# A searched order of steps replaced by another: same steps and buffers, other ORDER, SLOTS, ENGS and WARM tables

## The chip, the cores and the metric

The kernel runs on one core of a Trainium2 chip. A core has five engines with instruction streams of their own: TensorE (PE, matrix multiplication), VectorE (DVE), ScalarE (ACT), GpSimd (POOL) and SyncE (SP), which here only issues DMAs. Sixteen DMA engines move the data. The metric is the device time of one execution in microseconds (us). A profile of one further execution shows when each instruction ran on its engine.

## What is computed

Attention with a window, for 4 batches of 8 heads with 768 tokens and 64 elements a head, then a feed-forward layer on the 3072 tokens of 512 elements. The reference, cut to what matters:

```python
scores = scale * np.matmul(q, k.transpose(0, 1, 3, 2))
keep = is_global | is_local            # first 8 keys, and the last 96
scores = np.where(keep, scores + bias, -1000000000.0)
a = np.exp(scores - max); a = a / (np.sum(a) + 1e-09)
x = np.matmul(a, v)                    # heads side by side: 3072 x 512
...
h = x @ w_in                           # 512 -> 1024
solu = h * softmax(h)
ln = (solu - mean) / np.sqrt(var + 1e-06) * g_ln
return ln @ w_out                      # 1024 -> 512
```

## The kernel before

The kernel first writes down a plan: 1115 steps, each with the engines that may do it, what it depends on, which buffers it takes and frees, and a function that emits its instructions. Four tables at the top of the file then say all that the plan leaves open. ORDER is a permutation of the step numbers, and instructions are emitted in this order; so it fixes what stands behind what in each engine's stream, in SyncE's stream of DMA issues too. SLOTS gives the buffer that each step takes out of its pool, ENGS the engine where several may do a step, and WARM where matmuls that compute nothing are put in to keep TensorE busy. The tables were found by a search outside the file that plans with a duration for each step. Nothing of the search is in the file, and an engine waits for whatever its next instruction needs, at whatever time that comes.

```python
for n, i in enumerate(ORDER.split()):
    s = self.steps[int(i)]
    s["slot"] = [(t, int(next(slots))) for t in s["take"]]
    s["warm"] = warm.get(n, [])
    out.append(s)
```

The work of one batch, by steps and by the lines that the profile names:

- *Loads.* SyncE issues the DMAs for k and q of a pair of heads (L478, in batch 3 L485), v (L492, with its ends at L500 and its first rows at L507), the weights w_in (L608, four parts, into the buffer `late`) and w_out (L618, four parts). An engine casts them to 16 bits (L266 on ScalarE, L268 on VectorE, L270 on GpSimd).
- *Turning k and q.* In batches 0 to 2 TensorE transposes them (L726) and ScalarE or VectorE copies them from PSUM (L266, L268). In batch 3 SyncE issues DMA transposes for them (L760, tiles kT and qT), one for k and one for q of each of four pairs. The first 8 keys of every pair go through a small GpSimd step into the tile kg (L522).
- *Attention.* Scores by TensorE (L872, bias L858; the first keys L924 and L930), exponentials by ScalarE (L880, L937), sums (L951, L960), their logarithms (L967) spread by L1011 and exponentiated (L1020), the product with v (L1045, L1055), and the scaled result xT on VectorE (L1080). In batches 1 to 3 VectorE multiplies the exponentials by a factor (L888).
- *First layer.* For each of 24 tiles of 128 tokens eight matmuls of 512 columns (L1114) into two PSUM banks, ef = exp on ScalarE (L1120), then u = ef times the sum on VectorE (L1123), which frees the banks; squares of u on ScalarE (L1130) or VectorE (L1134). There are three buffers for u (uu0 to uu2) and two for ef.
- *Second layer.* u is transposed, for tiles 5 to 21 by a DMA that SyncE issues (L1139, into `late`), for the others by TensorE (L1149) and a copy; a buffer of u is free when its square and its transpose are done. Then eight matmuls of 512 columns (L1195), scaling (L1205 on ScalarE, L1208 on VectorE), and the store (L1212), issued by SyncE or ScalarE.
- *Weights.* w_out is scaled (L631, L637), and its mean (L644) taken off (L648) before the second layer.

Matmuls of line L1221 are those of WARM. SyncE's stream is the queue that the change's name speaks of: its DMA issues run one after the other, and an issue that has to wait holds up all behind it.

Of the kernel before, what the change touches and what calls it, by code (L numbers as in the profile page):

```python
# [28 lines left out]
FACT = {1, 2, 3}  # L29
SPLIT = False  # L30
ORDER = """
# [31 lines left out]
"""  # L63
SLOTS = """
# [10 lines left out]
"""  # L75
ENGS = """
# [4 lines left out]
"""  # L81
WARM = """
18:0:5 30:1:4 34:2:5 44:3:1 47:4:7 52:5:3 74:2:2 118:1:5 131:4:1 152:7:1 161:7:1 167:7:1
"""


# [1173 lines left out]
```

## Time and profile before

| what | us |
|---|---|
| median of 3 runs | 161.38 |
| lowest and highest run | 161.08 and 162.39 |
| the profiled execution's own time | 161.28 |
| its span, first to last instruction | 159.6 |

In the profile the span is the time from the first instruction of the program to the last; the run's time has 1.7 us around it. PE, DVE, ACT and POOL are the engines as above, PEld is TensorE's loading of weights, SPq is SyncE's queue of issues. The busy share of an engine is an average over stages; what bounds a stage is read from what its engines waited for there. The page's digits are busy tenths in 40 slices of 4 us.

### The profile page before, as it was taken

The page shows a single profiled execution, that of the slowest core. Times are in us where ns is not written, and L with a number is a line of the kernel's source. Part 1 is how long each engine was busy: PE and PEld are TensorE (multiplying, and loading weights), DVE is VectorE, ACT ScalarE, POOL GpSimd, SP SyncE. Part 2 cuts the span into 40 slices and gives each one's busy share as a digit, 9 for nine tenths or more (in the row PEclk, how much of TensorE's full clock was granted, in tenths as well). Part 3 has the DMA queues.
Part 4 walks back from the last instruction along what each step waited for, and adds up shares of the span by engine and source line. Part 5 has one row for each costly group of instructions (what it writes and reads, how often), then busy time and mean ns, then how long its engine had stood idle before and what let it go on. Part 6 is the DMA issues. An engine that isn't in the chain of part 4 may idle for free.

```text
span 159.6 us, 4825 instructions
## 1 busy us (share of the span) xinstructions
PE 147.4 (92%) x1893; PEld 79.8 (50%) x1893; DVE 114.0 (71%) x256; ACT 130.5 (82%) x219; POOL 56.4 (35%) x127
## 2 busy tenths in 40 slices
PE   5797989997999999999999799689999999999991
PEld 1454555455664556664444456334546644444550
DVE  6824778599998996889949976866975474728500
ACT  3949998999999799979897599768996679886531
POOL 7583935728756096400543042261040400000000
PEclk9999999999999999999999999999999999999998
DMA  4899989999999999999998999889972965681333
GB/s 152 249 347 331 317 229 359 349 373 334 366 313 263 217 193 266 257 193 205 246 186 180 242 189 191 164 217 198 227 236 82 172 148 113 184 229 66 134 138 131
DMA packets 74519, 35.85 MB, mean 225 GB/s; under 512 B 63608, under 2 KB 70016, under 8 KB 74496
## 3 DMA queue, kind: packets, MB, share of 16 engines
q1 hardware_dynamic: 73776, 34.22, 90.7%
q10 hardware_dynamic: 720, 1.31, 2.3%
q8 instruction: 15, 0.25, 0.7%
q14 instruction: 8, 0.07, 0.1%
HBM read 23.20 MB, written 6.29 MB: 185 GB/s over the span
## 4 chain that ended last, share of the span: by engine, by line
PE 59%; DMA 20%; DVE 6%; SPq 3%; POOL 3%; ACT 3%; issue 3%; DVEq 0%; ACTq 0%
PE acc L1195 24%; PE acc L1114 17%; DMA x<-in_q_dram 8%; DMA late<-in_moe_w_in_dram 4%; PE acc L1055 4%; DMA late<-uu 3%; DMA kT<-x 2%; PE acc L726 2%; DMA x<-in_k_dram 2%; DVE uu L1123 2%; PE acc L872 2%; PE acc L1149 2%; PE acc L951 2%; PE acc L1011 2%; POOL fb L325 1%
## 5 line engine op out<-in xcount | busy, mean ns | idle before, releaser
L1195 PE MATMUL acc<-gw_out_sb,late 128*128 128x512 f16 (+1 forms) x200 | 44.3, 371 | 0.0
L1114 PE MATMUL acc<-w_in_sb,xT 128*128 128x512 f16 x192 | 44.1, 380 | 0.2
L1123 DVE SCALAR_TENSOR_TENSOR uu<-ef,acc 128x1024 f16<-128x1024 f16 x24 | 29.1, 1217 | 13.2 <-ACT ef L1120 10.4
L880 ACT ACTIVATE eb<-acc 128x960 f16<-128x960 f32 (+1 forms) x32 | 29.3, 953 | 1.3 <-PE acc L872 1.2
L1195 PEld LDWEIGHTS <-late 128*128 128x128 f16 x200 | 18.9, 98 | 20.9 <-issue 0.7
L1120 ACT ACTIVATE ef<-acc 128x1024 f16<-128x1024 f32 x24 | 24.5, 1022 | 5.5 <-PE acc L1114 5.2
L1114 PEld LDWEIGHTS <-xT 128*128 128x128 f16 x192 | 18.1, 98 | 21.3 <-issue 0.6
L270 POOL CAST x<-x 128x768 f16<-128x768 f32 x18 | 15.1, 843 | 23.7 <-DMA x<-in_q_dram 11.3
L1130 ACT ACTIVATE sqa<-uu 128x1024 f16<-128x1024 f16 x20 | 21.2, 1058 | 0.3 <-DVE uu L1123 0.3
L1080 DVE TENSOR_TENSOR xT<-acc,rr 128x384 f16<-128x384 f32 x32 | 16.0, 551 | 5.7 <-ACT rr L1020 4.1
L270 POOL CAST v<-v 128x704 f16<-128x704 f32 (+3 forms) x16 | 10.0, 641 | 24.1 <-DMA v<-in_v_dram 24.1
L1205 ACT ACTIVATE osb<-acc,rstd 128x512 f32<-128x512 f32 (+1 forms) x18 | 12.1, 675 | 7.5 <-PE acc L1195 7.0
L888 DVE TENSOR_TENSOR eb<-eb,fb 128x960 f16<-128x960 f16 (+1 forms) x24 | 15.6, 674 | 2.1 <-POOL fb L325 1.8
L1055 PE MATMUL acc<-eb,v 64*64 64x160 f16 (+4 forms) x448 | 15.4, 220 | 0.0
L726 PE MATMUL acc<-ident,x 128*128 128x128 f16 x144 | 12.4, 228 | 2.9 <-ACT x L266 2.1
L872 PE MATMUL acc<-qT,kT 64*64 64x160 f16 (+2 forms) x384 | 12.6, 229 | 2.4 <-DMA kT<-x 1.3
L1020 ACT ACTIVATE rr<-acc 128x768 f32<-128x768 f32 x16 | 12.7, 812 | 2.6 <-PE acc L1011 2.0
L1055 PEld LDWEIGHTS <-v 64*64 64x64 f16 x448 | 12.8, 106 | 2.6 <-issue 1.7
L1221 PE MATMUL acc<-busy 128*128 128x512 f16 x36 | 12.1, 455 | 1.5 <-DVE busy L551 1.5
L726 PEld LDWEIGHTS <-x 128*128 128x128 f16 x144 | 9.2, 102 | 8.0 <-ACT x L266 3.8
L872 PEld LDWEIGHTS <-kT 64*64 64x64 f16 x384 | 8.8, 106 | 4.8 <-issue 2.1
L1045 PE MATMUL acc<-eg,vgz 64*64 64x384 f16 x64 | 10.8, 324 | 0.0
(116 smaller groups left out, 195.3 us busy)
## 6 DMA issues: line engine op xcount, KB each, us to landing
x<-in_k_dram SPq DMA_DIRECT2D x16, 384.0 KB, 4.8
x<-in_q_dram SPq DMA_DIRECT2D x16, 384.0 KB, 5.6
out_dram<-osb SPq DMA_DIRECT2D x18, 256.0 KB, 2.5
v<-in_v_dram SPq DMA_DIRECT2D x12, 192.0 KB, 4.6
late<-in_moe_w_in_dram SPq DMA_DIRECT2D x4, 512.0 KB, 5.7
w_out<-in_moe_w_out_dram SPq DMA_DIRECT2D x4, 512.0 KB
v<-in_v_dram SPq DMA_DIRECT2D x12, 160.0 KB, 4.5
out_dram<-osb ACTq DMA_DIRECT2D x5, 256.0 KB, 3.2
```

Source lines behind the costliest of these rows:

```text
L270: nc.gpsimd.tensor_copy(out=out, in_=in_)
L726: nc.tensor.transpose(out=pt[:, ts(j, P)], in_=a[:, j, ts(pp, P)], identity=ident)
L872: nc.tensor.matmul(out=sc[o : o + 64, par, col : col + n], lhsT=kk[r, BLK * c : BLK * c + BLK], rhs=qq[r, g0 : g0 + n], start=fresh, stop= ...
L880: ex["fn"] = (lambda ex=ex, qk=qk, gw=gw: nc.scalar.activation(out=eb[at(qk, "eb")][:, :, 0:gw], in_=big(qk)[:, :, 0:gw], func=AF.Exp, sca ...
L888: nc.vector.tensor_tensor(out=e, in0=e, in1=fb[:, p, :, 0:gw], op=ALU.mult)
L1055: nc.tensor.matmul(out=o_[64 * h : 64 * h + 64, gl : gl + m], lhsT=vv[r, v_at(vi, h, c), pair, :], rhs=view(eb[at(e_own[b, gi, pair], "eb" ...
L1080: nc.vector.tensor_tensor(out=xT[at(xt_own[b], "xT")][:, p, q0:q1], in0=one(av, d)[:, 0:w], in1=rr[at(re, "rr")][:, d, 0:w], op=ALU.mult)
L1114: nc.tensor.matmul(out=ph()[:, ts(fh, 512)], lhsT=xT[at(xt_own[b], "xT")][:, j, ts(t % NA, P)], rhs=w_in_sb[:, j, ts(fh, 512)], start=(j = ...
L1120: ex["fn"] = lambda g1=g1, t=t, ph=ph: nc.scalar.activation(out=ef[at(g1, "ef")], in_=ph(), func=AF.Exp, accum_out=s0[:, t : t + 1])
L1123: u["fn"] = lambda u=u, g1=g1, t=t, ph=ph: nc.vector.scalar_tensor_tensor(out=uu[at(u, "uu")], in0=ef[at(g1, "ef")], scalar=USC, in1=ph(), ...
L1130: nc.scalar.activation(out=sqs_["ACT"], in_=uu[at(u, "uu")], func=AF.Square, accum_out=s2[:, t : t + 1])
L1195: nc.tensor.matmul(out=one(g2)[:, 0:wd], lhsT=uT[at(el_o, "uT")][:, c, :], rhs=gw_out_sb[:, c, sl_], start=(c == 0), stop=(c == NFC - 1))
```

## The change

The plan, its steps, its buffers and every function that emits instructions stay as they are. The four tables are replaced by those of a new search. In that search, DMA issues of SyncE take longer when they fall beside a transfer of TensorE's instructions. The diff, with most rows of the tables left out:

```diff
 ORDER = """
-2 12 13 14 0 6 1 92 94 79 81 47 73 3 4 17 18 15 95 19 16 10 23 31 25 99 11 96 112 9 82 101 66 75 76
...
+2 13 105 11 12 3 18 73 112 4 107 6 19 1 0 45 66 68 114 75 14 17 5 76 69 115 8 20 133 77 86 88 89 90
...
 SLOTS = """
-0 0 0 1 1 1 2 0 3 4 1 2 0 5 3 1 0 0 2 1 2 0 1 2 3 0 0 1 4 3 3 3 0 0 3 1 0 1 2 2 2 3 3 3 3 2 4 2 0 2
...
+0 1 2 0 0 3 1 1 2 0 3 1 0 1 2 0 4 3 2 0 3 5 0 1 1 1 3 2 2 4 0 3 3 0 0 1 2 3 3 3 4 3 2 2 3 0 0 1 2 3
...
 WARM = """
-18:0:5 30:1:4 34:2:5 44:3:1 47:4:7 52:5:3 74:2:2 118:1:5 131:4:1 152:7:1 161:7:1 167:7:1
+23:0:14 24:1:7 32:3:1 54:5:1 62:5:1 64:5:2 111:2:1
```

By engine, the new ENGS table moves these: squares of u, 20 on ScalarE and 4 on VectorE before, 12 and 12 now; copies of turned k, 5 on ScalarE and 7 on VectorE before, 8 and 4 now; casts of k, 3 on ScalarE, 3 on VectorE and 10 on GpSimd before, 5, 6 and 5 now; casts of w_in, 2, 4 and 2 before, 3, 2 and 3 now; stores, 20 issued by SyncE and 5 by ScalarE before, 17 and 8 now. The WARM matmuls are 27 instead of 36.

The first place is ScalarE's stream at the start of the program, up to the first exponential of scores (L880). The rows give the line, the operation, and out<-in with buffer numbers; x32 is a load of k or q, x16 its cast. Before:

```order
L266 CAST x16_0_106<-x32_0_100 128x768
L266 CAST x16_1_107<-x32_1_101 128x768
L549 ACT_TABLE_LOAD
L266 COPY kT0_115<-acc_157 128x768
L266 CAST x16_2_108<-x32_3_103 128x768
L266 CAST x16_0_106<-x32_4_104 128x768
L266 CAST x16_1_107<-x32_5_105 128x768
L266 COPY kT1_116<-acc_157 128x768
L266 COPY qT0_120<-acc_157 128x768
L266 CAST x16_3_109<-x32_0_100 128x768
L320 ACTIVATE fb_166<-fx32_165 128x8x160
L880 ACTIVATE eb0_129<-acc_157 128x960
```

And now:

```order
L549 ACT_TABLE_LOAD
L266 CAST x16_1_107<-x32_3_103 128x768
L266 CAST x16_2_108<-x32_2_102 128x768
L266 CAST x16_3_109<-x32_4_104 128x768
L266 COPY qT2_122<-acc_157 128x768
L266 COPY kT0_115<-acc_157 128x768
L266 COPY kT2_117<-acc_157 128x768
L320 ACTIVATE fb_166<-fx32_165 128x8x160
L880 ACTIVATE eb0_129<-acc_157 128x2x448
```

Three casts of loads no longer stand ahead of the first exponential on ScalarE; other engines do them. The last of the three copies now belongs to the k of the third pair, whose load is the eighth issue on SyncE and the sixth load of k or q.

The second place is SyncE's stream where the DMA transposes of batch 3's k and q (L760) stand among the transposes of u (L1139), loads of v (L492, L500) and stores (L1212). Before:

```order
L760 DMA_TRANSPOSE kT4_119<-x16_2_108 128x6x128
L760 DMA_TRANSPOSE qT4_124<-x16_0_106 128x6x128
L492 DMA v32_2_112<-in_v_dram 128x6x64
L1139 DMA_TRANSPOSE late_153<-uu1_151 128x8x128
L760 DMA_TRANSPOSE kT0_115<-x16_1_107 128x6x128
L760 DMA_TRANSPOSE kT2_117<-x16_3_109 128x6x128
L760 DMA_TRANSPOSE qT1_121<-x16_2_108 128x6x128
L1139 DMA_TRANSPOSE late_153<-uu0_150 128x8x128
```

And now, from a little further ahead, the place where the transposes of the first three u tiles of this stretch stand:

```order
L760 DMA_TRANSPOSE qT3_123<-x16_2_108 128x6x128
L492 DMA v32_0_110<-in_v_dram 128x5x64
L492 DMA v32_1_111<-in_v_dram 128x5x64
L500 DMA vt32_88<-in_v_dram 64x4x64
L1139 DMA_TRANSPOSE late_153<-uu2_152 128x8x128
L1212 DMA out_0_dram<-osb0_154 128x512
L760 DMA_TRANSPOSE kT0_115<-x16_1_107 128x6x128
L1139 DMA_TRANSPOSE late_153<-uu0_150 128x8x128
L485 DMA x32_0_100<-in_q_dram 128x12x64
L1139 DMA_TRANSPOSE late_153<-uu1_151 128x8x128
```

Before, five of the eight L760 stand in this piece, three of them in a row, and the first two u transposes (a dozen rows ahead of it) follow each other directly. Now the L760 are spread over a longer piece, and a store and a k transpose stand between the first and the second u transpose.

The third place is ScalarE's stream that follows TensorE's scores of batch 3: L880 is the exponential of a pair's scores, L937 that of the first keys (which needs kg, and so the k transposes of all pairs), L1120 the ef of a first-layer tile, L1205 the scaling of a second-layer tile. Before:

```order
L1120 ACTIVATE ef0_148,s0_91<-acc_157 128x1024
L880 ACTIVATE eb3_132<-acc_157 128x960
L880 ACTIVATE eb1_130<-acc_157 128x960
L880 ACTIVATE eb2_131<-acc_157 128x960
L1120 ACTIVATE ef1_149,s0_91<-acc_157 128x1024
L1177 ACTIVATE vb_95<-va_94 128x3
L1178 ACTIVATE rstd_97<-vb_95 128x3
L1120 ACTIVATE ef0_148,s0_91<-acc_157 128x1024
L266 CAST v16_1_114<-v32_2_112 128x11x64
L937 ACTIVATE eg1_128<-acc_157,gbias_81 128x384
```

And now:

```order
L880 ACTIVATE eb6_135<-acc_157 128x960
L1177 ACTIVATE vb_95<-va_94 128x3
L1178 ACTIVATE rstd_97<-vb_95 128x3
L1120 ACTIVATE ef0_148,s0_91<-acc_157 128x1024
L880 ACTIVATE eb0_129<-acc_157 128x960
L880 ACTIVATE eb4_133<-acc_157 128x2x448
L1205 ACTIVATE osb0_154<-acc_157,rstd_97 128x512
L1130 ACTIVATE sqa_89,s2_93<-uu1_151 128x1024
L1205 ACTIVATE osb1_155<-acc_157,rstd_97 128x512
L880 ACTIVATE eb7_136<-acc_157 128x960
L880 ACTIVATE eb8_137<-acc_157 128x2x448
L937 ACTIVATE eg1_128<-acc_157,gbias_81 128x384
```

Before, the first keys' exponential came straight after the three first-layer tiles; now three second-layer tiles (two with their L1205 here, one scaled on VectorE) and two more exponentials of scores stand between.

86 rows, old and new, of tables (ENGS, ORDER, SLOTS) are left out of this document.

## The prediction

> **What bounds the kernel now.** I read the page's busy shares and slices first, then who waited for whom on TensorE, then stages by windows, then SyncE's own timeline.
>
> ```profile
> PE 147.4 (92%) x1893; PEld 79.8 (50%) x1893; DVE 114.0 (71%) x256; ACT 130.5 (82%) x219; POOL 56.4 (35%) x127
> PE   5797989997999999999999799689999999999991
> PEclk9999999999999999999999999999999999999998
> L1221 PE MATMUL acc<-busy 128*128 128x512 f16 x36 | 12.1, 455 | 1.5 <-DVE busy L551 1.5
> PE acc L872 <- DMA kT<-x: 1.3, 1, 1.3
> PE acc L1011 <- DVE uu L1123: 1.0, 1, 1.0
> PE acc L872 <- DVE uu L1123: 0.9, 1, 0.9
> PE acc L924 <- POOL kg L522: 0.5, 1, 0.5
> ```
>
> TensorE is busy 92% of the span and its granted clock is full to the last slice. Its work is the same in both kernels, so the time changes by what TensorE stands still, or fills with the empty matmuls of L1221. After the start only four waits matter, of 0.5 to 1.3 us, and three of them (L872 twice, L924) lie close together.
>
> ```profile
> 16.00:54.00 38.00, 35.80 (x617) 20.98 (x610) 32.80 (x63) 37.22 (x63) 22.31 (x41) 1.00 1.05 316
> 88.00:112.00 24.00, 21.28 (x309) 11.18 (x305) 17.89 (x39) 19.32 (x34) 6.85 (x10) 1.00 1.12 201
> ```
>
> These two stretches (length, then busy PE, PEld, DVE, ACT, POOL, then clock, DMA share, GB/s) say which engine bounds which stage. From 16 to 54 us ScalarE is busy 37.22 of 38: there it carries the time, and TensorE only keeps up. From 88 to 112 us TensorE loses 2.72 of 24 us, and no engine is full (ScalarE 19.32, VectorE 17.89): something is late.
>
> ```profile
> 78.47 3.73 SPq L1139 DMA_TRANSPOSE late<-uu  x2
> 85.55 1.26 SPq L1139 DMA_TRANSPOSE late<-uu  x1
> 86.90 0.53 SPq L1212 DMA_DIRECT2D out_dram<-osb  x1
> 91.31 1.84 SPq L760 DMA_TRANSPOSE kT<-x  x1
> 97.19 2.91 SPq L760 DMA_TRANSPOSE kT<-x  x2
> 83.42 1.22 DVE L1123 SCALAR_TENSOR_TENSOR uu<-ef,acc 128x1024 f16<-128x1024 f16 x1 [1.79 <-DMA late<-uu]
> 89.00 0.40 PE L872 MATMUL acc<-qT,kT 64*64 64x160 f16 x12 [0.86 <-DVE uu L1123]
> 101.32 0.40 PE L872 MATMUL acc<-qT,kT 64*64 64x160 f16 x12 [1.28 <-DMA kT<-x]
> 103.81 0.34 PE L924 MATMUL acc<-qT,kg 128*32 128x384 f16 x1
> 105.30 1.04 PE L1114 MATMUL acc<-w_in_sb,xT 128*128 128x512 f16 x4
> 71.77 0.35 PE L924 MATMUL acc<-qT,kg 128*32 128x384 f16 x4
> 72.35 0.39 PE L1114 MATMUL acc<-w_in_sb,xT 128*128 128x512 f16 x1
> ```
>
> What is late comes from SyncE. An undisturbed transpose issue takes 1.26 us; the two u transposes from 78.47 on take 3.73 together, a k transpose 1.84. The u step at 83.42 had waited 1.79 us for the first of them, to have its buffer free. The PSUM banks of the u steps behind it are what the scores at 89.00 wait for (0.86 us). The scores at 101.32 wait 1.28 us for a k transpose itself. The first keys' products, started at 103.81, let the next tile start at 105.30, 1.49 us later; the same twelve matmuls in the batch before took 71.77 to 72.35, or 0.58, so 0.91 is lost to the tile kg, made from the turned k.
>
> ```profile
> q8 instruction: 15, 0.25, 0.7%
> 19.44 2.14 SPq L492 DMA_DIRECT2D v<-in_v_dram  x1
> 22.63 1.70 SPq L608 DMA_DIRECT2D late<-in_moe_w_in_dram  x1
> 21.63 0.49 SPq L608
> GB/s 292 317 276 287 302 418 301 292 255 254 289 297 239 324 282 365 328 338 335 299 295 261 208 152 75 62 41 43 68 189 275 371 128 126 230 236 265 317 265 399
> q8 instruction: 2, 0.03, 2.4%
> ```
>
> TensorE's instructions come in 15 packets on queue q8: its 1893 matmuls and 1893 weight loads over 15 are 252 a packet. Between 18 and 24 us two such packets fall, and in the same six us two issues take 2.14 and 1.70 us where their like takes 0.49. The GB/s of that window (40 slices of 0.15 us) sink from about 300 to 41: while SyncE is held, the DMA engines run dry. So the plan's new rule names something that this trace shows.
>
> The Trainium skill, "Runtime: NRT & Kernel Launch", section "Instruction fetch mechanics", says that an engine's instructions are refilled in blocks of 256 over a queue of its own, and that the cost of crossing a block is mostly hidden. By that rule no issue of SyncE would be longer for it; the block size agrees with the 252 above, the hidden cost does not agree with 2.14 against 0.49.
>
> **The change part by part.** The sum is made against the profiled execution, 161.28 us (span 159.6 and 1.7 around it); the median of the runs, 161.38, is 0.1 above it, so nothing is added for that.
>
> *Batch 3's transposes and first keys.* The transposes take as long as before and are as many, but they are issued earlier against those who need them. The L937 of the first keys now stands behind three second-layer tiles and two more scores. A second-layer tile is eight matmuls like the L1195 group's:
>
> ```profile
> 90.33 1.83 PE acc L1195 x8
> 28.91 0.71 POOL w_in_sb L270
> 156.25 0.47 ACT osb L1205
> L1134 DVE SCALAR_TENSOR_TENSOR sqv<-uu 128x1024 f16<-128x1024 f16 x4 | 4.9, 1223 | 0.1
> ```
>
> Three of them are 5.5 us. That is more than the waits of 1.28 and 0.91 that end there, with two held issues of the sizes above, 1.65 and 1.2, on top. The wait of 0.86 goes if the u transposes land in time: the first one now stands behind three loads that need nothing late. So I count 0.86 + 1.28 + 0.91 = 3.05 us as gained. Bounds: nothing gained, if the same holds fall elsewhere; 4.0 us if the wait of 1.0 on L1011 goes as well. I take 3.0, since three separate rows say what ended each wait and all three are eased in the new rows. Late next is then the u step itself, which follows ScalarE's ef.
>
> *ScalarE's start.* Here ScalarE bounds, so its first exponential sets when it can be done.
>
> ```profile
> 11.25 0.83 ACT L266 CAST x<-x 128x768 f16<-128x768 f32 x1 [1.22 <-DMA x<-in_q_dram]
> 12.30 0.83 ACT L266 CAST x<-x 128x768 f16<-128x768 f32 x1 [0.22 <-DMA x<-in_k_dram]
> 14.42 0.84 ACT L266 CAST x<-x 128x768 f16<-128x768 f32 x1
> 15.15 1.28 ACT L320 ACTIVATE fb<-fx 128x1280 f16<-128x1280 f32 x1
> 16.32 4.36 ACT L880 ACTIVATE eb<-acc 128x960 f16<-128x960 f32 x5
> L880 ACT ACTIVATE eb<-acc 128x960 f16<-128x960 f32 (+1 forms) x32 | 29.3, 953 | 1.3 <-PE acc L872 1.2
> L266 ACT COPY kT<-acc 128x768 f16<-128x768 f16 x5 | 4.0, 790 | 0.1
> L1130 ACT ACTIVATE sqa<-uu 128x1024 f16<-128x1024 f16 x20 | 21.2, 1058 | 0.3 <-DVE uu L1123 0.3
> ```
>
> Between the first exponential and the fourth ef the new order has on ScalarE two casts (0.83), two k copies (0.79), one exponential (0.95), a half-size cast (0.6 by half the size and a fixed part) and a copy of 1024 columns (1.05, the 0.79 by width) more, a q copy (0.8) and three squares (1.06, and 0.2 to the next start) less: 1.66 + 1.58 + 0.95 + 0.6 + 1.05 - 0.8 - 3.8 = 1.2 us more. So the first exponential must start by 16.32 - 1.2 = 15.1 to be no later at the end. It now waits for the sixth load of k or q. The sixth landed at 12.3 before (the cast there was released by its landing), with three small loads ahead, now two. From there: a cast on VectorE 0.5, six transposes 0.5, ScalarE's copy 0.8, the table exponential 1.2 to its next start (15.15 to 16.32), and some 0.1 at each of the hand-overs: 15.4. So 0.3 us is lost. Bounds: -0.7 (landing 1 us earlier, for the small loads) and +2.0 (one more load of 1.0 us, the step from 11.25 to 12.30, ahead of it, and a held issue of 1.2 less slack).
>
> *w_in.* Its last part was in use at 28.91, straight after landing. In the new order its last issue stands behind one part of w_out more, 0.5 MB: at the 316 GB/s of the first window 1.7 us later. Against it stand the two held issues above, 1.65 and 1.2 us over their like, which the new plan allows for. Between -1.0 and +1.7 I take nothing: either way its cover is ScalarE's backlog until 54 us.
>
> *VectorE.* Eight squares more at 1.2 us are 9.8 us, on an engine with 6 us idle in the 24 of the second window and more behind it. I cost it at nothing; without that cover, a square ahead of a u step costs 1.2 us. *Empty matmuls*, 27 for 36: nothing, they fill waits for loads. *Stores* moved between SyncE and ScalarE: nothing; the end (0.47 us of scaling, then the last store) is the same.
>
> Sum: 161.3 - 3.0 + 0.3 = 158.6 us, 1.7% under the median.
>
> **The rivals.** *The order gives back what it gains.* The holds follow TensorE's instructions, one in about 252, not the plan's clock; where execution drifts by 1 to 2 us from the plan, they fall on other issues, and another L760 or u transpose is late. For it: all four waits above are about 1 us, the size of one hold. Against it: the new rows leave 5.5 us more ahead of the first keys. It gives 161.3. The rule of the Trainium skill above ("Runtime: NRT & Kernel Launch", "Instruction fetch mechanics") would come to the same time by another way: with no hold to plan for, the two searches would be worth the same.
>
> *Slower: the second u transpose.* Before, the first two u transposes followed each other; now a store (0.53, as at 86.90) and a k transpose (1.26) stand between, so the second lands 1.8 us later behind the first u of the stretch. If each of the two transposes there is held once more, by 1.2, it is 4.2 us. A u step waits for its buffer, its PSUM banks come free later, and the wait of 0.86 becomes 5. Then 161.3 - 2.2 (the other two waits) + 0.3 + 4.2 = 163.6. It decides from 3.6 us on, where the time passes 163.0. For it: the u step at 83.42 waits in this way already. Against it: it takes two holds in a row.
>
> **How the numbers follow.** I give 0.50 to the forecast, 158.6, 0.30 to the order giving back, 161.3, and 0.20 to the slower rival, 163.6. One per cent, 1.6 us, is about what a measurement of this kernel can tell from no change, so faster means under 159.8 and slower over 163.0. Each case lies in one of these: faster 0.50, same 0.30, slower 0.20. The forecast's own range is 161.3 - 4.0 - 0.7 = 156.6 to 160.2 (half the waits left). With the second case and its w_in bound of +1.7 the range reaches to 163.0, and leaves out the slower rival and the tail below: 156.6 to 163.0.
>
> **What would show it.** Right: TensorE's waits for kT, kg and for u behind a u transpose are gone or under 0.3 us, and TensorE idles under 0.7 us between 88 and 112 us; ScalarE's first L880 starts at 14.6 to 16. Held issues of 2 us on SyncE are still there, but no chain runs through them. Wrong: a wait of TensorE over 1 us in the middle of the program on anything from SyncE; a first L880 after 17.3; the first L1114 after 32.

## The result and the profile after

| what | before | after |
|---|---|---|
| median, 20 runs each | 162.17 us | 159.81 us |
| the profiled execution's own time | 161.28 us | 158.86 us |
| its span | 159.6 us | 157.2 us |
| TensorE idle from 54 to 150 us | 2.78 us | 0.56 us |

The ratio is 0.9877, with a 95% interval of 0.9849 to 0.9905: the changed kernel is 1.2% faster. Some runs of nearly every kernel here are slow, over 1.5% above its fastest: the ratios leave them out, a profile taken in one has a star in the table of the experiments, and idle time is compared between those without.

The windows from 54 to 150 us, of before, of after, and of one more profile of the changed kernel (length, busy PE, PEld, DVE, ACT, POOL, then clock, DMA share, GB/s):

```profile
54.00:150.00 96.00, 93.22 (x1159) 49.15 (x1157) 71.65 (x156) 80.34 (x143) 24.32 (x32) 1.00 0.96 189
```

```profile
54.00:150.00 96.00, 95.44 (x1148) 49.69 (x1146) 76.22 (x164) 78.80 (x142) 24.11 (x32) 1.00 0.93 188
```

```profile
54.00:150.00 96.00, 95.45 (x1148) 49.76 (x1147) 76.11 (x164) 78.80 (x142) 23.89 (x32) 1.00 0.93 188
```

TensorE idles 2.78 us before and 0.56 and 0.55 after. The spans are 159.6, 157.2 and 157.4. So 2.2 of the 2.2 to 2.4 us that the span lost lie in this stretch, and the start, up to 54 us, and the tail together gave at most 0.2 us.

The same window that the prediction showed of before, from 88 to 112 us, and below it the only wait of TensorE over 0.2 us between 54 and 152 us in the profile after:

```profile
88.00:112.00 24.00, 23.67 (x327) 12.23 (x327) 19.32 (x42) 20.09 (x34) 4.28 (x7) 1.00 1.16 215
```

```profile
88.33 0.26 PE L1055 MATMUL acc<-eb,v 64*64 64x160 f16 x4 [0.55 <-DVE uu L1123]
```

The idle time of this window fell from 2.72 to 0.33 us. The waits for kT, for kg and for the u behind a held transpose are gone. What is left is a wait of 0.55 us on a u step.

SyncE's timeline after, the issues that stand where the first transposes of u and the k and q transposes of batch 3 are:

```profile
77.47 1.25 SPq L1139 DMA_TRANSPOSE late<-uu  x1
78.78 0.57 SPq L1212 DMA_DIRECT2D out_dram<-osb  x1
79.46 1.27 SPq L760 DMA_TRANSPOSE kT<-x  x1
80.83 1.57 SPq L1139 DMA_TRANSPOSE late<-uu  x1
...
90.71 2.11 SPq L760 DMA_TRANSPOSE kT<-x  x1
...
94.90 1.21 SPq L760 DMA_TRANSPOSE kT<-x  x1
...
102.38 1.30 SPq L760 DMA_TRANSPOSE qT<-x  x1
...
109.57 3.92 SPq L1139 DMA_TRANSPOSE late<-uu  x2
```

Issues are still held (2.11 at 90.71, 3.92 for two at 109.57), and no wait of TensorE hangs on them. The last k transpose is issued at 94.90; before, it was the second of the two from 97.19 on. Before, the 43 issues that begin between 60 and 106 us run from 60.52 to 108.10 with no gap over 0.11 us between two of them: SyncE never waited for anyone, its queue was full. In the changed kernel its stream pauses twice, for 1.10 us at 60.17 and 0.61 at 76.86. From 77.47 to 112 us its issues follow each other without a gap as before. So a full queue alone does not tell the two kernels apart where the waits were. What differs there is what stands in the queue at which place, and how far off its users are.

### The profile page after: what moved, and what is told of

Read it like the earlier page. It is cut to its first block, busy times and chain, and to the rows that moved or that the text cites. A ratio compares the mean times of both kernels' runs of the same rounds, so it can differ in the third digit from the quotient of the medians.

```text
span 157.2 us, 4813 instructions
## 1 busy us (share of the span) xinstructions
PE 145.1 (92%) x1884; PEld 79.6 (51%) x1884; DVE 124.1 (79%) x268; ACT 125.0 (80%) x208; POOL 57.2 (36%) x125
## 4 chain that ended last, share of the span: by engine, by line
PE 69%; DVE 12%; DMA 8%; ACT 4%; POOL 3%; issue 1%; DVEq 0%; POOLq 0%
PE acc L1195 27%; PE acc L1114 22%; PE acc L1055 6%; DMA late<-in_moe_w_in_dram 4%; DMA x<-in_k_dram 4%; DVE uu L1123 3%; DVE eb L888 3%; PE acc L872 3%; PE acc L726 2%; DVE xT L1080 2%; PE acc L1011 2%; PE acc L1149 2%; PE acc L951 2%; ACT eb L880 2%; PE acc L1045 1%
## 5 line engine op out<-in xcount | busy, mean ns | idle before, releaser
L1114 PE MATMUL acc<-w_in_sb,xT 128*128 128x512 f16 x192 | 44.1, 379 | 0.1
L1120 ACT ACTIVATE ef<-acc 128x1024 f16<-128x1024 f32 x24 | 24.8, 1031 | 8.1 <-PE acc L1114 8.0
L880 ACT ACTIVATE eb<-acc 128x896 f16<-128x896 f32 (+1 forms) x32 | 28.7, 954 | 1.8 <-PE acc L872 1.7
L1114 PEld LDWEIGHTS <-xT 128*128 128x128 f16 x192 | 18.0, 98 | 21.5 <-issue 1.1
L1055 PE MATMUL acc<-eb,v 64*64 64x160 f16 (+3 forms) x448 | 15.8, 221 | 1.5 <-DVE tick L1065 0.8
L974 POOL TENSOR_SCALAR lhi<-lns,mlo 128x384 f16<-128x384 f32 x5 | 6.3, 1258 | 29.8 <-ACT lns L967 28.7
L888 DVE TENSOR_TENSOR eb<-eb,fb 128x960 f16<-128x960 f16 (+1 forms) x24 | 16.0, 690 | 0.8 <-ACT eb L880 0.8
L1205 ACT ACTIVATE osb<-acc,rstd 128x512 f32<-128x512 f32 x16 | 11.0, 688 | 6.3 <-PE acc L1195 6.2
L1134 DVE SCALAR_TENSOR_TENSOR sqv<-uu 128x1024 f16<-128x1024 f16 x12 | 15.4, 1283 | 0.1
L726 PE MATMUL acc<-ident,x 128*128 128x128 f16 x144 | 11.9, 224 | 1.2 <-DVE x L268 0.6
L1130 ACT ACTIVATE sqa<-uu 128x1024 f16<-128x1024 f16 x12 | 12.8, 1066 | 0.0
L266 ACT CAST x<-x 128x768 f16<-128x768 f32 x8 | 6.5, 837 | 6.0 <-DMA x<-in_k_dram 6.0
L872 PEld LDWEIGHTS <-kT 64*64 64x64 f16 x384 | 9.3, 108 | 3.6 <-issue 2.5
```

The source lines that it names most:

```text
L726: nc.tensor.transpose(out=pt[:, ts(j, P)], in_=a[:, j, ts(pp, P)], identity=ident)
L872: nc.tensor.matmul(out=sc[o : o + 64, par, col : col + n], lhsT=kk[r, BLK * c : BLK * c + BLK], rhs=qq[r, g0 : g0 + n], start=fresh, stop= ...
L880: ex["fn"] = (lambda ex=ex, qk=qk, gw=gw: nc.scalar.activation(out=eb[at(qk, "eb")][:, :, 0:gw], in_=big(qk)[:, :, 0:gw], func=AF.Exp, sca ...
L888: nc.vector.tensor_tensor(out=e, in0=e, in1=fb[:, p, :, 0:gw], op=ALU.mult)
L1055: nc.tensor.matmul(out=o_[64 * h : 64 * h + 64, gl : gl + m], lhsT=vv[r, v_at(vi, h, c), pair, :], rhs=view(eb[at(e_own[b, gi, pair], "eb" ...
L1114: nc.tensor.matmul(out=ph()[:, ts(fh, 512)], lhsT=xT[at(xt_own[b], "xT")][:, j, ts(t % NA, P)], rhs=w_in_sb[:, j, ts(fh, 512)], start=(j = ...
```

## The experiments

All ratios are to the kernel before, run on the same chip in turn. Idle is TensorE's, of the 96 us from 54 to 150.

| run | ratio | 95% interval | idle, us |
|---|---|---|---|
| the changed kernel again | 0.9869 | 0.9823 to 0.9915 | 0.55 |
| changed, packets shifted | 0.9834 | 0.9767 to 0.9901 | 1.26* |
| changed, two stores back on SyncE | 0.9896 | 0.9835 to 0.9957 | 1.27* |
| changed, first keys early | 0.9924 | 0.9875 to 0.9973 | 3.47* |
| changed, squares back | 1.0341 | 1.0263 to 1.0418 | 4.72 |
| changed, searched on | 1.034 | 1.0232 to 1.0447 | 6.67* |
| before, packets shifted | 0.9991 | 0.9939 to 1.0044 | 1.97* |
| before, two issues moved | 0.9979 | 0.9936 to 1.0022 | 4.06 |
| before, first keys later | 1.0009 | 0.9947 to 1.007 | 2.14 |
| before, three stores on ScalarE | 0.9891 | 0.9829 to 0.9954 | 1.75 |
| before, three stores and first keys later | 0.9978 | 0.9921 to 1.0035 | 2.28 |
| before, SyncE's stream eased | 1.0015 | 0.9945 to 1.0085 | 3.70* |

**The changed kernel again**, unchanged.

> The changed kernel itself, on the same chip as the three others of this set. All theories: ratio 0.985 to 0.991 to the kernel before, TensorE idle for under 1 us between 54 and 150 us.

It came as expected; the gain is the same in another set of runs.

**Does the gain hang on where TensorE's instruction packets fall?** In both kernels the first 27 empty matmuls are cut in three, so that TensorE's stream has 54 matmuls more ahead of its real work, which moves the packets against it:

```diff
+    split = 27
     for s in plan.order():
         for spot, count in s["warm"]:
             for _ in range(count):
-                nc.tensor.matmul(out=acc[:, spot, :], lhsT=busy16[:, 0:P],
-                                 rhs=busy16, start=True, stop=True)
+                cuts = (0, 128, 320, 512) if split > 0 else (0, 512)
+                split -= 1
+                for c0, c1 in zip(cuts, cuts[1:]):
+                    nc.tensor.matmul(out=acc[:, spot, c0:c1], lhsT=busy16[:, 0:P],
+                                     rhs=busy16[:, c0:c1], start=True, stop=True)
```

> The changed kernel; each of its 27 empty matmuls of 512 columns is written as three of 128, 192 and 192 columns. The columns computed are the same, but TensorE's stream has 54 matmuls and 54 weight loads more ahead of its real work, so its instruction packets (one in about 126 matmuls) fall about half a packet earlier in the work. Theory 1 (the new order is good because the issues that are held have nobody waiting close behind): other issues are now held, and 1 to 2 us of the gain go: ratio to the kernel before 0.994 to 1.000, with a wait of TensorE or VectorE over 0.8 us on something of SyncE between 60 and 112 us. Theory 2 (the gain is the longer distance between transposes and their users, wherever the holds fall): ratio 0.985 to 0.991 as unshifted, no such wait.

> The kernel before; its first 27 empty matmuls are split in the same way, 54 matmuls and weight loads more ahead of the real work. The holds should leave the issues of 67.53 (2.95 us), 78.47 (2.05) and 113.33 (2.45) and appear on others beside the new packet times, which shows that packets and not these issues make them. Theory 1: the order was not made for any packet times, so the time moves little either way, ratio 0.996 to 1.004 (a u transpose is no longer held at 78, other issues are). Theory 2: the same time, ratio 0.998 to 1.002. A rival to both, that the holds come from the DMAs themselves: the long issues stay where they were.

The packets did not move by one amount. Counted in real matmuls that start ahead of a packet, the four of the changed kernel between 80 and 112 us moved by 22 to 64; of the five of the kernel before from 67 to 99 us, two stayed and three moved by 22 to 79. The changed kernel kept its gain (0.9834), and between 60 and 112 us no wait of TensorE over 0.8 us came, nor one of VectorE on SyncE. Theory 1 is out as far as this shift goes: this order does not need its packets at one place. In the kernel before, other issues were held now. SyncE's timeline, first of before unshifted, then shifted (the first two rows are the same two loads in both):

```profile
66.24 1.23 SPq L485 DMA_DIRECT2D x<-in_q_dram  x1
67.53 2.95 SPq L500 DMA_DIRECT2D vt<-in_v_dram  x1
```

```profile
68.00 2.40 SPq L485 DMA_DIRECT2D x<-in_q_dram  x1
70.45 1.42 SPq L500 DMA_DIRECT2D vt<-in_v_dram  x1
...
80.99 2.94 SPq L1139 DMA_TRANSPOSE late<-uu  x2
...
93.00 3.15 SPq L760 DMA_TRANSPOSE kT<-x  x1
```

The load of v's ends (L500) that took 2.95 us takes 1.42, the two u transposes of 3.73 us take 2.94; now the load of q takes 2.40 instead of 1.23 and the k transpose that took 1.84 takes 3.15, with packets at 67.7 and 93.2 us. These long issues stand beside the packets again. The time did not move (0.9991): TensorE again waited for a k transpose (0.90 us) and for kg (0.80 us).

**Are the waits worth their sum?** Two edits of the kernel before, each of which takes away waits at 101 to 105 us. The first is in SyncE's stream alone:

```diff
 L760 DMA_TRANSPOSE qT_124<-x_0_106 128x6x128
-L492 DMA v_2_112<-in_v_dram 128x6x64
-L1139 DMA_TRANSPOSE late<-uu_151 128x8x128
 L760 DMA_TRANSPOSE kT_115<-x_1_107 128x6x128
 L760 DMA_TRANSPOSE kT_117<-x_3_109 128x6x128
+L1139 DMA_TRANSPOSE late<-uu_151 128x8x128
 L760 DMA_TRANSPOSE qT_121<-x_2_108 128x6x128
+L492 DMA v_2_112<-in_v_dram 128x6x64
```

> The kernel before; in SyncE's stream alone one load of v (L492) goes behind the last of batch 3's k and q transposes that followed it, and one u transpose (L1139) behind the two k transposes, so these two k transposes are issued 1.2 to 2.5 us earlier. As the prediction summed it: the waits of 1.28 us (L872 on kT) and 0.91 us (first keys on kg) go and the time falls by 2.2 us, ratio 0.986. Rival: both waits go, but what stands next (u transposes needed by the second layer at 110 us, and u behind ScalarE and VectorE) ends only 0.5 us earlier: ratio 0.997, with new waits of TensorE between 108 and 116 us.

The wait for kT went, and others took its place (TensorE's timeline of that run):

```profile
89.99 0.40 PE L872 MATMUL acc<-qT,kT 64*64 64x160 f16 x12 [0.76 <-DVE uu L1123]
...
104.88 0.40 PE L872 MATMUL acc<-qT,kT 64*64 64x160 f16 x12 [1.81 <-DMA qT<-x]
...
112.11 1.90 PE L1195 MATMUL acc<-gw_out_sb,late 128*128 128x512 f16 x8 [0.76 <-DMA late<-uu]
```

TensorE now waits 1.81 us for a q transpose and, at 112.11, 0.76 for a u transpose, both issued by SyncE behind what was moved ahead. The time is the same (0.9979), not 2.2 us less. The rival's size was right; the waits stand partly at 105 us and not only from 108.

The second edit is in TensorE's stream alone (ScalarE's two L937 stood far enough back already):

```diff
-first keys: L924 and L930 of both groups
 first layer, one tile: L1114 x8
 second layer, one tile: L1195 x8
+first keys: L924 and L930 of both groups
```

> The kernel before; the first keys of batch 3 (L924, L930, then L937) behind one first-layer and one second-layer tile (3.7 us of TensorE), which followed them before; the other engines' streams as they were, apart from the place of the two L937. The prediction's step alone (distance between the last transposes and their users): the wait of 0.91 us goes, ratio 0.994. Rival (the work behind stands still for the same queue: u transposes that SyncE issues behind the k and q transposes): the wait moves to L1195 or L1011, ratio 0.998 to 1.002.

Again no gain (1.0009). The first keys wait no more, but the scores ahead of them do, and the second-layer tile behind:

```profile
101.27 0.40 PE L872 MATMUL acc<-qT,kT 64*64 64x160 f16 x12 [1.59 <-DMA kT<-x]
...
110.13 1.90 PE L1195 MATMUL acc<-gw_out_sb,late 128*128 128x512 f16 x8 [0.42 <-DMA late<-uu]
```

The wait of 0.86 us for the u step, at 89 us, is not in this profile either, though no engine's stream differs from that of before ahead of 103 us. So waits of this size come and go from one execution to the next, and one profile does not give them their price.

**Is it SyncE's full queue?** Three stores of the kernel before go from SyncE to ScalarE:

```diff
 SyncE, between the transposes of 85 to 91 us:
-L1212 DMA out_dram<-osb_154 128x512
-L1212 DMA out_dram<-osb_155 128x512
-L1212 DMA out_dram<-osb_156 128x512
 ScalarE, behind its ef steps there:
+L1212 DMA out_dram<-osb_156 128x512
+L1212 DMA out_dram<-osb_155 128x512
+L1212 DMA out_dram<-osb_154 128x512
```

> The kernel before; three stores (L1212), which SyncE issued among the transposes between 86 and 91 us, are issued by ScalarE behind its next ef steps; nothing else is changed. SyncE's stream is without a gap from 60 to 109 us in the trace of before, so each store there costs its 0.43 to 0.53 us. Theory 3 (SyncE's queue is full from 60 to 109 us, and what the new order gains is that this queue ends earlier): the k and q transposes come 1.4 us earlier and the time falls by about 1.2 us, ratio 0.993. The prediction's step that stores moved between the two engines bring nothing: ratio 0.998 to 1.002.

It was 1.1% faster (between 0.5 and 1.7%), and TensorE's idle time fell by 1.0 us, near the 1.2 expected. The plain means of the runs compared, 161.3 and 162.1 us, give only 0.5%. One wait was left, for a u transpose:

```profile
92.56 1.90 PE L1195 MATMUL acc<-gw_out_sb,late 128*128 128x512 f16 x8 [1.61 <-DMA late<-uu]
```

With the first keys later as well:

> The kernel before with both small edits: three stores issued by ScalarE and the first keys later. If the two add up: 1.2 + 0.9 us, ratio 0.987, as the changed kernel. If only the shorter queue counts: as with the three stores alone, ratio 0.989 to 0.994.

The ratio is 0.9978, with an interval that leaves out the whole gain of the changed kernel and overlaps that of the three stores alone. So what three stores are worth is not settled between 0.2 and 1.1%; the two edits do not add up to the change.

The other way round, in the changed kernel, the two stores that ScalarE issues at 75.13 and 97.89 us go back to SyncE:

> The changed kernel; the two stores that ScalarE issues between 75 and 98 us are issued by SyncE at their places in the order. Theory 3, where the queue is full: two issues of 0.5 us are 1 us, ratio 0.992 to 0.996. If the queue of the changed kernel has room (it has 4.5 us of gaps between 60 and 106 us): as the changed kernel, 0.985 to 0.991.

The ratio, 0.9896, lies within what the changed kernel gives itself: two issues more do it no clear harm, though the interval reaches into what theory 3 expected. The 4.5 us of gaps are no such room: counted in the same way the kernel before has 3.1 us, the short pauses between any two issues, and the only longer ones in the changed kernel are the 1.10 and 0.61 us above.

Then the stream of SyncE in the kernel before as a whole: between 54 and 125 us its issues in another order, and four stores on ScalarE (its core; loads of v, k and q change places too):

```diff
 SyncE, 86 to 101 us:
-L1212 three stores
 L760 DMA_TRANSPOSE kT (pair 2)
+L760 DMA_TRANSPOSE kT (pair 3)
 L760 DMA_TRANSPOSE qT (pair 3)
-L492 one load of v
+L760 DMA_TRANSPOSE kT (pair 0)
 L1139 DMA_TRANSPOSE late<-uu
-L760 DMA_TRANSPOSE kT (pair 3)
-L760 DMA_TRANSPOSE kT (pair 0)
 L760 DMA_TRANSPOSE qT (pair 0)
```

> The kernel before; SyncE's stream between 54 and 125 us in another order (k and q transposes ahead of loads that are needed later), and four stores of this stretch issued by ScalarE. The streams of TensorE, VectorE and GpSimd are word for word those of before, ScalarE's has only the four stores more. Theory 3: SyncE's queue alone makes the loss, so nearly all of the gain of the changed kernel comes, 1.5 to 2.2 us, ratio 0.986 to 0.991, with no wait of TensorE over 0.5 us between 80 and 112 us. Rival (the gain needs TensorE's own new order, users farther from their transposes): under 0.8 us, ratio 0.995 to 1.0.

No gain (1.0015): the strong form of theory 3, that SyncE's order and fewer issues in it bring the gain by themselves, is not borne out. It is no clean test of an emptier queue, since even with four stores less no gap over 0.12 us came between 54 and 112 us. TensorE stands still at another place:

```profile
88.68 3.38 PE L1195 MATMUL acc<-gw_out_sb,late 128*128 128x512 f16 x8 [2.13 <-DMA late<-uu]
```

These eight matmuls take 3.38 us and not 1.90 because TensorE's granted clock was 0.5 for 3.41 us from 88.94 on; the wait came ahead of that.

**Undoing one part of the change.** In the changed kernel the first keys go ahead of the three second-layer tiles again:

```diff
+first keys: L924 and L930 of both groups, L937 of each
 second layer, three tiles: L1195 x24
 scores: L872 of two pairs
-first keys: L924 and L930 of the first group, L937
 first layer, two tiles: L1114 x16
-first keys: L924 and L930 of the second group, L937
```

> The changed kernel; the first keys of batch 3 (L924, L930 and their exponentials L937) stand ahead of the three second-layer tiles again and not behind them. The prediction's step: those tiles cover the last q and k transposes, so without them TensorE waits there, 1 to 2 us, and the time is that much longer: ratio 0.994 to 1.002. Rival (the tiles cover nothing, since the transposes come earlier anyway): as the changed kernel, 0.985 to 0.991.

TensorE waits there, for the last q transpose:

```profile
105.06 0.38 PE L872 MATMUL acc<-qT,kT 64*64 64x160 f16 x12
108.05 0.51 PE L924 MATMUL acc<-qT,kg 128*32 128x384 f16 x4 [2.61 <-DMA qT<-x]
```

The ratio is 0.9924, half a per cent above the changed kernel, though the intervals overlap; the plain means of the runs compared, 161.9 and 162.1 us, put it next to the kernel before. The tiles do cover a late transpose, and it is one of q: the k transposes and kg were done at 100.52.

The squares of u go back to the engines that did them before, in the changed order:

```diff
 ENGS, by squares of u:
-12 on ScalarE, 12 on VectorE
+20 on ScalarE, 4 on VectorE
```

> The changed kernel; the squares of u are done by the engines that did them before (20 on ScalarE, 4 on VectorE), the order is kept. The prediction's step (squares on VectorE cost or bring nothing): within 0.5 us of the changed kernel, ratio 0.985 to 0.991. Rival (the order is tight on ScalarE, and an engine can't be changed in it without moving others): 3 to 8 us slower than the changed kernel, ratio 1.005 to 1.04, with TensorE's new waits on ScalarE's ef or VectorE's u.

It is 3.4% slower than the kernel before, 4.7% than the changed one. The groups of VectorE's u step, in the changed kernel and in this run (busy, mean ns | idle before, and what ended it):

```profile
L1123 DVE SCALAR_TENSOR_TENSOR uu<-ef,acc 128x1024 f16<-128x1024 f16 x24 | 29.1, 1217 | 6.6 <-ACT ef L1120 6.1
```

```profile
L1123 DVE SCALAR_TENSOR_TENSOR uu<-ef,acc 128x1024 f16<-128x1024 f16 x24 | 29.2, 1218 | 15.5 <-ACT ef L1120 15.3
```

The u steps wait 15.3 us for ef instead of 6.1: squares stand in ScalarE's stream ahead of the ef that the next u needs.

**Searching on.** A version whose order and engines were changed further so that a replay of the changed kernel's trace, with every measured duration and landing kept, ended earlier:

> The changed kernel; order and engines searched a little further by replaying the trace of the changed kernel with every duration and hold as measured there. In the replay it ends 1.9 us earlier. If durations and holds stay where they were: ratio to the kernel before 0.975. Rival (holds and landings move with the order, so what a replay finds on one trace isn't found on the chip): ratio 0.985 to 1.0.

It is 3.4% slower than before. Two of TensorE's longest waits of that run:

```profile
4.56 0.82 PE L726 MATMUL acc<-ident,x 128*128 128x128 f16 x6 [4.56 <-POOL sf L309]
...
45.58 0.62 PE L1149 MATMUL acc<-ident,uu 128*128 128x128 f16 x8 [2.36 <-DVE uu L1123]
```

Neither is in the profile of the changed kernel. What ended earlier with one trace's durations and landings did not do so on the chip. No run here is clearly faster than the changed kernel.

## Why the prediction was right, and where its sizes were off

*The bound.* It said that TensorE's standstill between 88 and 112 us makes the difference and that SyncE is what is late. The first holds: the window's idle time fell by 2.39 us, which is the gain. The second holds in the main: each edit of the kernel before showed TensorE waiting for yet another transpose of SyncE's (kT, qT or u). One wait, that for kg, has a second cause, told below.

*The term of 3.0 us.* The three waits are gone, and the gain was 2.2. The term was mis-sized in two ways. The prediction's own window had 2.72 us of idle in it, so 3.05 could not be gained there. The 0.91 was read from two starts, between which TensorE was partly busy; its timeline of before has 0.50 there:

```profile
104.65 0.51 PE L924 MATMUL acc<-qT,kg 128*32 128x384 f16 x3 [0.50 <-POOL kg L522]
```

0.86 + 1.28 + 0.50 is 2.64. And a wait came in, 0.55 us at 88.33, on the u step, which the prediction had named as what is late next without giving it a price. 2.64 - 0.55 is 2.1, what was measured to 0.1.

*Why the waits for kT and kg went.* The prediction priced the cover by three second-layer tiles, 5.5 us. Below are the steps that make kg, before, with VectorE's work beside them, and then in the changed kernel:

```profile
102.60 2.17 POOL L522 TENSOR_TENSOR kg<-kT,hpick 128x16 f16<-128x16 f16 x4 [4.83 <-DMA kT<-x]
102.16 1.22 DVE L1134 SCALAR_TENSOR_TENSOR sqv<-uu 128x1024 f16<-128x1024 f16 x1
103.31 1.21 DVE L888 TENSOR_TENSOR eb<-eb,fb 128x896 f16<-128x896 f16 x2
```

```profile
98.00 0.76 POOL L522 TENSOR_TENSOR kg<-kT,hpick 128x16 f16<-128x16 f16 x4 [4.67 <-DMA kT<-x]
```

In the changed kernel kg is done at 98.76 and its first user starts at 110.21. The tiles take 5.35 of these 11.4 us, so kg would have been in time without them: the k transposes come earlier. What the tiles cover is the last q transpose, for which the forecast had no term. And kg was late before for a reason besides SyncE: its four small steps took 2.17 us and not 0.76, since each of the first three ended only just after a VectorE instruction beside it had ended. At 0.76 they would have been done at 103.36, ahead of the 103.81 at which the first keys' products start.

*That the three waits are gained one by one.* The sum came near with the whole order changed. Taken alone the steps bring no gain that can be seen: two issues moved, 0.9979 instead of the 0.986 of the sum; the first keys later, 1.0009 instead of 0.994. What was moved ahead in the full queue made late what stood there. The cover of three second-layer tiles is real in the changed kernel (2.61 us of waiting without it). Which places of the new order together bring the gain was not separated.

*The holds.* The rival that the order gives its gain back, because holds drift, did not come about: shifting the packets on purpose took nothing away. Issues of 2 us are still there and no wait hangs on them, as the prediction asked for. The Trainium skill, "Runtime: NRT & Kernel Launch", section "Instruction fetch mechanics", has the cost of a block's crossing mostly hidden. What it costs TensorE itself no run here shows; SyncE's issues beside a packet are longer (numbers below), so for this kernel the measurement decides against taking it as nothing. Its rule would have made the two orders worth the same, and they are not; but since the shifted kernel kept the gain, that difference doesn't show that planning for the holds is what brought it.

*The slower rival.* The second u transpose took 1.57 us at 80.83 and was not held by two packets in a row; the u steps had their buffers.

*ScalarE's start.* A loss of 0.3 us was forecast, from a first exponential at 15.4. It came at 14.22, earlier than the 14.6 to 16 that were named as a sign of being right:

```profile
8.78 1.58 ACT L266 CAST x<-x 128x768 f16<-128x768 f32 x2
...
11.65 1.51 ACT L266 COPY kT<-acc 128x768 f16<-128x768 f16 x2
13.05 1.28 ACT L320 ACTIVATE fb<-fx 128x1280 f16<-128x1280 f32 x1
14.22 4.37 ACT L880 ACTIVATE eb<-acc 128x896 f16<-128x896 f32 x5
```

The term that was off is the landing of the sixth load: VectorE's cast of it starts at 11.21 (L268, 0.54 us), so it had landed at least 1.1 us before the 12.3 that was taken, near the end of the range called -0.7. It brought next to nothing by 54 us: start and tail together gave at most 0.2 us.

*w_in at nothing.* Its casts end later now and the first L1114 starts at 31.76 and not 30.08, 1.7 us later, which was the upper bound (31.49 in the other profile). It cost nothing that shows by 54 us.

*Squares at nothing* is right for this order and wrong as a statement on squares: the same ones moved without a new order cost 4.7%, some 7.5 us. *Stores at nothing* stays open: with them on ScalarE the kernel before was 1.1% faster in one set and 0.2% in another with a second edit. *Empty matmuls and tail*: nothing, as said.

*The time.* 158.6 was forecast from a median of 161.38; in the 20 runs the kernel before has 162.17, and the changed one 159.81. As a ratio it was 0.983, and 0.9877 was measured; as a difference of medians, 2.8 us and 2.4. The line that the prediction drew for faster, 159.8, came from the lower median of before, and 159.81 lies on it.

## What to carry to other kernels

Before adding up waits that a new order removes, hold their sum against the idle time of the bounding engine in that stretch: no more can come back. Look then at whether the queue they come from is full without a gap: if so, an issue moved ahead can make another one late, as here. The order that gained had a queue just as full at that place, with the transposes that were late issued earlier and with work between others and their users, at several places at once. Look also at every step between the transfer and its user: here small GpSimd steps were part of the wait. An engine or a place exchanged singly in a searched order says little of what it costs when the order is searched with it.

## What the runs showed of the hardware

*Issues of SyncE beside TensorE's instruction packets.* Over the 14 profiles of this case, between 15 and 130 us, an issue that has a packet between 0.8 us before its start and 0.3 us after its end takes on average 0.53 us longer than the median of its line in that profile (303 issues, 133 of them over 0.5 us longer); the others 0.04 us (1199 issues, 79 over 0.5). In each single profile the means were 0.38 to 0.79 and 0.01 to 0.08. So a packet near an issue makes it longer in under half the cases, and some long issues have no packet near them; what decides it was not found.

*Small GpSimd steps beside VectorE.* The last four steps L522 (128x16) take 0.21 to 0.23 us each in 11 of the 14 profiles. In the three others they fall beside VectorE's squares (L1134) and factors (L888), and the first three take 0.52 to 1.29, 0.59 and 0.62 us; each ends within 0.1 us after the VectorE instruction that ran when it started. That it is these VectorE instructions that hold them is read from these times and was not tested.
